# A decode layer on one core: five loop trips instead of four, a shorter TensorE program, 128 rows of w_down on 32 partitions, and unused products in TensorE's waits

## The chip, the cores and the metric

One core of one Trainium2 chip runs the kernel. The time is that of one execution on the device in microseconds (us). Times of the kernel before are the median of three runs; a profile is of one execution, whose own time is given beside its span.

The core has a matrix engine (TensorE, PE in the profile; PEld is its loading of weights), VectorE (DVE), ScalarE (ACT), GpSimd (POOL) and SyncE (SP), which here only issues transfers. Transfers run on sixteen DMA engines. Each engine follows its own program, and they wait for each other through semaphores.

## The reference

One step of decoding for two sequences: attention with a cache, then a gated feed-forward network, each behind a normalization and with its input added back. All arrays are bf16.

```python
B, Sq, D = 2, 1, 640;  Hq, Hkv, Sk, Dh = 32, 32, 8192, 192;  F = 1536
W = min(4096, max(256, Sk // 4))                     # 2048
xn = layernorm(x)
q = (xn @ wq).reshape(B, Sq, Hq, Dh).transpose(0, 2, 1, 3)
k, v = k_cache[:, :, Sk - W:, :], v_cache[:, :, Sk - W:, :]
p = softmax(einsum("bhqd,bhkd->bhqk", q, k) * Dh ** -0.5)
o = einsum("bhqk,bhkd->bhqd", p, v)
h = x + o.transpose(0, 2, 1, 3).reshape(B, Sq, Hq * Dh) @ wo
hn = layernorm(h)
out = h + (gelu(hn @ w_gate) * (hn @ w_up)) @ w_down
```

The last 2048 positions of K and V are read for each of 2 x 32 heads: 50.3 MB each. wq and wo are 7.9 MB each, w_gate, w_up and w_down 2.0 MB each.

## The kernel before

**Groups.** The 64 pairs of sequence and head are worked off in sixteen groups of four (`g`). A group is one K load and one V load of 3 MB each on 128 partitions: a partition holds 64 positions of one head, 24,576 bytes. Four groups form a round `J`, after which eight heads of both sequences are done.

**One group.** `transposes(g, half)` turns K by products with an identity (L574), six batches into four PSUM banks, which VectorE and ScalarE empty into `ktr` (L588, L584). `scores(g)` (L635) multiplies by the masked queries `rq`; VectorE finds the maxima (L644), a small product with `pm` (L651) spreads them, and ScalarE takes the exponentials (L655), all in `softmax`. `e_columns(g)` turns the exponentials into columns (L664), which VectorE masks into `ering`. `pv(g)` (L680) multiplies these with V and adds over the four groups of a round in the bank `ops`.

**The end of a round.** `z_rows` sums the exponentials, `o_rows` gathers the rows of the output through `osb` into the bank m1 (in the last round into `sps`), VectorE scales them into `orow`, `o_columns` (L713) turns them into columns `ot`, and `oproj(J)` (L731) multiplies with wo(J) into m1; VectorE adds the result to `hrow`.

**The queue of loads.** SP issues every large load (L363) in one fixed order. All of them share a ring of six slots of 24,576 bytes per partition: four for K (`K_AT`), two for V (`V_AT`), and other weights in slots that are free by then. A load is issued when the last reader of its bytes is done, so K waits for transposes and V for `pv`. wo(0) and wo(1) are loaded behind V of groups 3 and 7, wo(2) and wo(3) behind V of group 15, then w_gate, w_up and w_down. The first of five parts of w_gate and the two rows of x are issued by ScalarE at the start.

**The loop.** TensorE and VectorE run a loop of four trips; the other engines' programs are written out. Group 0's transposes, the queries (`q_rows`, L598, `q_stationary`) and group 0's scores and softmax stand ahead of it. A trip holds four groups as segments a to d; group `4J+p` does the first half of its transposes, `e_columns(g-1)`, the second half, `pv(g-1)`, its scores and its softmax. `o_columns` and `oproj` of the round before stand in segment a, under conditions on the trip, and the last trip leaves out d. The end of group 15, the last round, `oproj(2)` and `oproj(3)` stand behind the loop. Since a wait in the loop is a register that grows by a fixed step with each trip, every semaphore that is waited for there must be raised equally often in each trip; operations that don't fit get a semaphore class of their own (`cls`, `RARE`).

**The feed-forward part** follows `oproj(3)`. `h_columns` turns h into columns, `ffn_in` (L822) multiplies the normalized columns with w_gate, then w_up: for each of five parts of D, four products of 384 columns, one for each group of 32 columns of the array. `ffn_columns` (L831) turns the 98 x 384 results back into columns by three products of 128 columns, VectorE multiplies gelu's output with w_up's into `uT`, and 48 products (L871) with w_down in four pieces `WDC`, the last of one row per partition, end in m1. Each partition holds twelve rows of w_down. VectorE copies m1 to `yrow` (L877), and SP stores it.

## Time and profile before

| | us |
|---|---|
| median of 3 runs (292.71 to 292.77) | 292.76 |
| the profiled execution | 292.58 |
| its span | 291.3 |
| PE busy | 198.6 |
| DVE busy | 122.8 |
| ACT busy | 76.9 |
| POOL busy | 25.7 |
| DMA moved, mean over the span | 420 GB/s |

The span is from the first to the last instruction; the difference to the time lies around it. Busy time is the sum of an engine's instructions, and a busy engine isn't necessarily the bound. The mean granted clock of TensorE was 0.871 of full speed. Two more rows, from the costliest groups and from who waited for whom: the transposes (L574) took 116.2 us of TensorE's time in 768 products, and its products sat idle for 25.2 us until a K load landed. SP waited 130.5 us for `pv`, 35.4 us for transposes and 39.7 us for `oproj` before it could issue the next load.

### The profile page before, as it was taken

Reading aid. Unit: us, or ns where it says so; the run is one execution under the profiler, and the core shown is the slowest. Engines: PE = TensorE matmul, PEld = TensorE weight load, DVE = VectorE, ACT = ScalarE, POOL = GpSimd, SP = SyncE. Lnnn points to the kernel's source line nnn. Section 1 sums busy time; section 2 is a strip of 40 time slices with the busy share of each in tenths; the row PEclk is TensorE's granted clock in tenths of the full one; section 3 lists DMA queues with packets and bytes.
Section 4 is the critical chain, followed back from the end, with each engine's and each line's share of the span. In section 5 each row is a group of like instructions: output and inputs, shape, how many; then the busy total and the mean of one; then the engine's idle time right before and its main releaser. Section 6 shows DMA issues by size and latency. Waiting matters only on the chain.

```text
span 291.3 us, 5093 instructions
## 1 busy us (share of the span) xinstructions
PE 198.6 (68%) x2141; PEld 147.6 (51%) x2141; DVE 122.8 (42%) x231; ACT 76.9 (26%) x72; POOL 25.7 (9%) x85
## 2 busy tenths in 40 slices
PE   0650868786668288768677478868478778496684
PEld 0640437566355175637374475645465746472341
DVE  4350025455435334635356244635247445253331
ACT  1050014333322122423222123523142333151001
POOL 8820073000000000000000000000000000000000
PEclk9997568999979869997989579999689799688957
DMA  8999999999999999999999999999999999999994
GB/s 324 432 440 422 428 432 432 428 429 429 428 419 440 432 432 432 429 432 432 432 416 448 432 432 430 432 412 429 432 432 425 422 432 432 429 432 434 420 411 181
DMA packets 6506, 122.44 MB, mean 420 GB/s; under 512 B 734, under 2 KB 864, under 8 KB 1504
## 3 DMA queue, kind: packets, MB, share of 16 engines
q1 hardware_dynamic: 6348, 121.90, 97.8%
q10 hardware_dynamic: 148, 0.40, 0.4%
q8 instruction: 7, 0.11, 0.2%
q14 instruction: 3, 0.02, 0.0%
HBM read 122.29 MB, written 0.00 MB: 420 GB/s over the span
## 4 chain that ended last, share of the span: by engine, by line
DMA 73%; PE 18%; DVE 3%; issue 2%; SPq 2%; ACT 1%; DVEq 0%
DMA ring<-in_A_k_cache_dram 54%; PE tpp L574 13%; DMA ring<-in_A_wq_dram 10%; DMA ring<-in_B_w_down_dram 9%; DVE ktr L588 3%; PE tpp L598 2%; SPq L363 2%; PE ops L680 1%; DVE ering L428 1%; ACT ktr L584 1%; PE m L731 1%; PE m L713 1%; PE m L871 0%; PE m L694 0%; DVE yrow L877 0%
## 5 line engine op out<-in xcount | busy, mean ns | idle before, releaser
L574 PE MATMUL tpp<-identf,ring 128*128 128x128 f32 x768 | 116.2, 314 | 39.3 <-DMA ring<-in_A_k_cache_dram 25.2
L574 PEld LDWEIGHTS tpp<-identf,ring 128*128 128x128 f32 x768 | 102.8, 163 | 47.5 <-DMA ring<-in_A_k_cache_dram 26.5
L588 DVE COPY ktr<-tpp 128x2048 bf16<-128x2048 bf16 x64 | 78.4, 1224 | 91.4 <-PE tpp L574 91.4
L584 ACT ACTIVATE ktr<-tpp 128x2048 bf16<-128x2048 bf16 x32 | 60.1, 1877 | 94.9 <-PE tpp L574 94.9
L655 ACT ACTIVATE eexp<-sm,nm 128x512 bf16<-128x512 f32 x16 | 11.6, 722 | 71.7 <-DVE nm L653 71.7
L635 PE MATMUL sps<-ktr,rq 128*16 128x512 bf16 x384 | 25.7, 402 | 1.1 <-POOL rq L428 1.1
L680 PE MATMUL ops<-ring,ering 128*32 128x384 bf16 x512 | 25.0, 339 | 0.0
L644 DVE CUSTOM_DVE_ANT_1 sm<-sps,mska 128x512 f32<-128x512 f32 x16 | 11.0, 686 | 27.0 <-issue 27.0
L428 POOL TENSOR_TENSOR rq<-qs,mask 128x96 bf16<-128x96 bf16 x16 | 5.5, 354 | 175.6 <-PE sps L635 154.1
L680 PEld LDWEIGHTS ops<-ring,ering 128*32 128x32 bf16 x512 | 12.7, 99 | 8.5 <-issue 2.8
L635 PEld LDWEIGHTS sps<-ktr,rq 128*16 128x16 bf16 x384 | 8.9, 89 | 14.4 <-issue 5.5
L651 PEld LDWEIGHTS m<-mrhs,pm 128*128 128x128 bf16 x16 | 1.5, 96 | 22.9 <-DVE mrhs L424 22.9
L651 PE MATMUL m<-mrhs,pm 128*128 128x16 bf16 x16 | 2.9, 184 | 14.8 <-DVE mrhs L424 14.8
L598 PE MATMUL tpp<-ring,xnT 128*32 128x384 bf16 x80 | 6.1, 499 | 9.4 <-DMA ring<-in_A_wq_dram 9.4
L598 PEld LDWEIGHTS tpp<-ring,xnT 128*32 128x32 bf16 x80 | 3.4, 143 | 11.9 <-issue 9.6
L621 DVE CAST qs<-ops 128x384 bf16<-128x384 f32 x1 | 0.6, 558 | 15.8 <-PE ops L616 15.8
L428 DVE TENSOR_TENSOR ering<-m,mask 128x256 bf16<-128x256 f32 x16 | 6.6, 415 | 1.3 <-PE m L664 1.3
L713 PE MATMUL m<-selb,orow 128*128 128x2 bf16 x48 | 3.5, 200 | 5.2 <-DVE ering L428 4.5
L713 PEld LDWEIGHTS m<-selb,orow 128*128 128x128 bf16 x48 | 3.2, 159 | 6.0 <-DVE ering L428 4.9
L664 PE MATMUL m<-sel,eexp 128*128 128x64 bf16 x64 | 4.8, 200 | 1.2 <-ACT eexp L655 1.2
L494 PE MATMUL m<-identb,xrow 2*128 2x2 bf16 x5 | 0.3, 173 | 7.4 <-DMA xrow<-in_A_x_dram 7.4
L428 DVE TENSOR_TENSOR orow<-m,wm 128x1536 bf16<-128x1536 f32 x3 | 5.3, 1751 | 0.0
(127 smaller groups left out, 93.6 us busy)
## 6 DMA issues: line engine op xcount, KB each, us to landing
ring<-in_A_k_cache_dram SPq DMA_DIRECT2D x16, 3072.0 KB, 29.5
ring<-in_A_v_cache_dram SPq DMA_DIRECT2D x16, 3072.0 KB, 25.4
ring<-in_A_wq_dram SPq DMA_DIRECT2D x1, 7680.0 KB, 28.1
ring<-in_A_wo_dram SPq DMA_DIRECT2D x4, 1920.0 KB, 21.6
ring<-in_B_w_gate_dram SPq DMA_DIRECT2D x1, 1536.0 KB, 31.4
ring<-in_B_w_up_dram SPq DMA_DIRECT2D x1, 1536.0 KB, 21.9
ring<-in_B_w_down_dram SPq DMA_DIRECT2D x1, 960.0 KB, 24.3
ring<-in_B_w_down_dram SPq DMA_DIRECT2D x1, 480.0 KB, 25.0
```

What stands on the lines that cost most here:

```text
L363: P.op("sp", lambda e, v=v, src=src: e.dma_start(v, src), W=toks + [("sem", sem)], dma=sem)
L428: return lambda e: e.tensor_tensor(out=out, in0=a, in1=b, op=op)
L574: ins = e.transpose(tpp[bi][:, 512 * j + 128 * u:512 * j + 128 * (u + 1)], kv[:, off:off + 128], identf[:, :])
L584: act(lambda e, dst=dst, bv=bv: e.activation(out=dst, in_=bv, func=ACT.Copy), W=[("kt", half, k)], X=both)
L588: dve(lambda e, dst=dst, bv=bv: e.tensor_copy(dst, bv.rearrange("p (a x) -> p a x", a=2)), W=[("kt", half, k)], X=both, cls=0)
L598: ins = e.matmul(tps[0][32 * r:32 * (r + 1), 0:384], lhsT=xnT[:, c, 32 * J:32 * (J + 1)], rhs=wq[:, c, 1536 * J + 384 * r:1536 * J + 384 * ...
L635: ins = e.matmul(sps[32 * ch:32 * ch + 16, :], lhsT=rq[:, g % 4, k, :], rhs=ktr[:, k // 2, 1024 * ch + k % 2:1024 * (ch + 1):2], start=(k ...
L644: dve(lambda e: e.tensor_tensor_reduce(out=sm[:, :].rearrange("p (u x) -> p u x", u=4), in0=sps[:, :].rearrange("p (u x) -> p u x", u=4), ...
L655: act(lambda e: e.activation(out=eexp[:, :], in_=sm[:, :], func=ACT.Exp, bias=nm[:, 0:1], scale=1.0, accum_out=zr[:, g % 4:g % 4 + 1]), R= ...
L664: ins = e.matmul(o, lhsT=eexp[:, 128 * u:128 * (u + 1)], rhs=sel64[:, :], start=True, stop=True)
L680: ins = e.matmul(ops_[32 * r:32 * (r + 1), 0:384], lhsT=ering[:, g % 4, t, :], rhs=vv[:, 384 * t:384 * (t + 1)], start=(g % 4 == 0 and t < 4),
L713: ins = e.matmul(m2[:, 2 * kk:2 * kk + 2], lhsT=orow[:, :, kk:DH:12], rhs=selb[:, :], start=True, stop=True)
```

## The change

**Loop and program.** The loop has five trips. Trip J below 4 does all transposes of group 4J, then (in trip 0) the queries, later the scores and softmax of groups 4J to 4J+3 with what lies between. Trip J above 0 first ends the round before: `e_columns` and `pv` of group 4J-1, `z_rows`, `o_rows`, `oproj(J-2)`, `o_columns(J-1)`. What stood ahead of the loop and behind it for groups 0 and 15 is gone from there; only `oproj(3)` stays behind.

**Semaphores.** The counts of classes 1 and 2 on TensorE and VectorE start from a bias of 16 with their first rise, the count of `wo` from 32 by an increment that GpSimd makes, so that a register's value stays above zero in every trip. More operations get classes of their own.

**Loads.** wo(0), wo(1) and wo(2) are issued behind V of groups 7, 11 and 15. wo(2) lies in the fourth K slot, w_up in the third. w_down's last 128 rows are a load of their own, `wds`, four rows for each of partitions 0 to 31, ahead of eleven rows for every partition in pieces of five, three, two and one.

**Products.** `ffn_in` splits the fourth product into one of 256 and one of 128 columns, `ffn_columns` has nine products instead of three (the last four for the 128 rows on 32 partitions), `uT` has sixteen columns of pairs instead of twelve. w_down takes 16 products with `wds` and 44 instead of 48 with the rest. `o_rows` writes to m2. `keep_busy(n)` multiplies the identity with `qrow` n times into a bank where nothing reads it.

```diff
-RARE = ("oc", "op")
+BIAS = 16
+WO_BIAS = 32
+RARE = ("oc", "q", "y0")
...
-        if eng == "pe" and self.seg in RARE:
+        if self.seg == "op" and eng in LOOPED:
+            cls = 2
+        elif eng == "pe" and self.seg in RARE:
             cls = 1
...
-            ins.then_inc(sems[o.key()], 1)
+            ins.then_inc(sems[o.key()], 1 + BIAS if o.cls in (1, 2) and o.idx == 1 and o.eng in LOOPED else 1)
...
-WDC = ((0, 6), (6, 9), (9, 11), (11, 12))
+WDC = ((0, 5), (5, 8), (8, 10), (10, 11))
+NS = 11
...
-WO_AT = (K_AT[3], K_AT[3], K_AT[2], 0)
+WO_AT = (K_AT[3], K_AT[3], K_AT[3], 0)
+WU_AT = K_AT[2]
+WDS_AT = K_AT[1] + 12288
...
-            wd = B_w_down.rearrange("(q p s) n -> q p s n", p=128, s=6)
+            load("wds", WDS_AT, 8 * D, B_w_down[128 * NS:F, :].rearrange("(c a u) n -> a c (u n)", a=8, u=4), lambda v: v[0:32, :], "wds")
+            wd = B_w_down[0:128 * NS, :].rearrange("(p s) n -> p s n", s=NS)
...
-            if g % 4 == 3 and g < NG - 5:
-                load_wo(g // 4)
-        load_wo(2)
+            if g % 4 == 3 and g > 3:
+                load_wo(g // 4 - 1)
         load_wo(3)
...
+        def keep_busy(n, bank=tps[1], tok=("t", 1)):
+            def fn(e):
+                for k in range(n):
+                    ins = e.matmul(bank, lhsT=identb[:, :], rhs=qrow[:, :, :, :].rearrange("p a b d -> p (a b d)")[:, 0:bank.shape[1]],
+                                   start=True, stop=True, skip_group_check=True)
+                return ins
+
+            pe(fn, R=["identb", "qrow"], X=[tok])
...
+        for J in range(5):
+            if J < 4:
+                P.loop_seg("d0", J)
+                transposes(4 * J, 0)
+                transposes(4 * J, 1)
+            if J == 0:
+                P.loop_seg("q", J)
+                q_rows()
+                q_stationary()
+            else:
+                P.loop_seg("y0", J)
+                e_columns(4 * J - 1)
+                z_rows(J - 1)
+                pv(4 * J - 1)
+                keep_busy(3, m1[:, 0:DH], "m1")
+                o_rows(J - 1)
+            if J > 1:
+                P.loop_seg("op", J)
+                keep_busy(2, m1[:, 0:DH], "m1")
+                oproj(J - 2)
+            if J > 0:
+                P.loop_seg("oc", J)
+                o_columns(J - 1)
+            if J < 4:
+                P.loop_seg("a0", J)
+                scores(4 * J)
+                softmax(4 * J)
+                for g in range(4 * J + 1, 4 * J + 4):
+                    transposes(g, 0)
+                    e_columns(g - 1)
+                    transposes(g, 1)
+                    pv(g - 1)
+                    scores(g)
+                    if g == 4 * J + 3:
+                        keep_busy(4, m1[:, 0:DH], "m1")
+                    softmax(g)
+                    if g == 4 * J + 3:
+                        keep_busy(6, m1[:, 0:DH], "m1")
         P.loop_seg()
-        e_columns(15)
-        z_rows(3)
-        pv(15)
-        o_rows(3)
-        oproj(2)
-        o_columns(3)
+        keep_busy(1)
         oproj(3)
+        keep_busy(2)
...
+                        for r in range(3):
+                            e.matmul(bank[32 * r:32 * r + 2, 0:384], lhsT=hnT[:, c, :], rhs=cols[:, :, 3 * r:3 * r + 3],
+                                     start=(c == 0), stop=(c == NC5 - 1), tile_position=(0, 32 * r))
+                        e.matmul(bank[96:98, 0:256], lhsT=hnT[:, c, :], rhs=cols[:, :, 9:11], start=(c == 0), stop=(c == NC5 - 1),
+                                 tile_position=(0, 96), skip_group_check=True)
+                        ins = e.matmul(bank[96:98, 256:384], lhsT=hnT[:, c, :], start=False,
+                                       rhs=wv[:, c - l0, 128 * NS:F].rearrange("p (c a u) -> p a c u", c=4, a=8),
+                                       stop=(c == NC5 - 1), tile_position=(0, 96), skip_group_check=True)
...
-                    ins = e.transpose(bank[:, 128 * j:128 * j + 98], row[0:98, j:384:3], identf[0:98, 0:98])
+                    e.transpose(bank[:, 128 * j:128 * j + 66], row[0:66, j:384:3], identf[0:66, 0:66])
+                for j in range(2):
+                    e.transpose(bank[:, 128 * j + 96:128 * j + 98], row[96:98, j:256:2], identf[96:98, 96:98])
+                for u in range(4):
+                    ins = e.transpose(bank[0:32, 384 + 32 * u:386 + 32 * u], row[96:98, 256 + u:384:4], identf[96:98, 96:98])
...
+        order = [(None, 4, ["d0", (None, 1, ["q"])]), (0, None, ["y0", (1, None, ["op"]), "oc"]), (None, 4, ["a0"])]
+        P.emit_loop("dve", nc.vector, sems, 5, order)
+        P.emit_loop("pe", nc.tensor, sems, 5, order)
```

More of the change, by code (lines that the diff above doesn't have):

```diff
@@ L159, in resolve @@
         for e, l in self.per.items():
-            n = {}
+            n = {c: BIAS for c in (1, 2) if e in LOOPED}
             for o in l:
@@ L607, in q_rows @@
                 in_=tps[0][:, 0:384].rearrange("p (h d) -> p h d", h=2).unsqueeze(2).to_broadcast([128, 2, 2, DH]),
-                func=ACT.Copy, scale=SCALE), W=["qrow"], X=[("t", 0)])
+                func=ACT.Copy, scale=SCALE), W=["qrow"], X=[("t", 0)], cls=1)
         def q_stationary():
@@ L752, in h_columns @@
             pe(fn, R=["hrow", ("hsel", 0), ("hsel", 1)], X=["m2"])
-        transposes(0, 0)
-        transposes(0, 1)
-        q_rows()
-        q_stationary()
         consts_late()
-        scores(0)
-        softmax(0)
-        for J in range(4):
-            for p in range(1, 5 if J < 3 else 4):
-                g = 4 * J + p
-                seg = "abcd"[p - 1]
-                P.loop_seg(seg + "0", J)
-                transposes(g, 0)
-                e_columns(g - 1)
-                if p == 4:
-                    z_rows(J)
-                if p == 1 and J > 0:
-                    P.loop_seg("oc", J)
-                    o_columns(J - 1)
-                P.loop_seg(seg + "1", J)
-                transposes(g, 1)
-                if p == 1 and 0 < J < 3:
-                    P.loop_seg("op", J)
-                    oproj(J - 1)
-                P.loop_seg(seg + "2", J)
-                pv(g - 1)
-                scores(g)
-                if p == 4:
-                    o_rows(J)
-                softmax(g)
@@ L819, in fn @@
                     for c in range(c0, c1):
[L820 to L823 removed]
+                        cols = wv[:, c - l0, 0:128 * NS].rearrange("p (x s) -> p x s", s=NS)
+                        for r in range(3):
[6 more added lines that the diff above has]
+                                       stop=(c == NC5 - 1), tile_position=(0, 96), skip_group_check=True)
                     return ins
@@ L863, in bass_sequential_preLN__sliding_block_cached__geglu_ffn__decode_kernel, with wds_rows @@
         vT = ffn_columns(urow, [("osb", 0), ("osb", 1)], tps[1], 1)
-        dve(tt(uT[:, :, 0:17:16].rearrange("p (r j) b -> p r j b", r=4), vT, rjb(ga[:, 0, :]), ALU.mult), R=["ga0"], W=["uT"], X=[("t", 1)])
+        dve(tt(uT[:, :, 0:17:16], vT, kb(ga[:, 0, :]), ALU.mult), R=["ga0"], W=["uT"], X=[("t", 1)])
+        wds, wtoks = where["wds"]
+        def wds_rows(e):
+            for u in range(4):
+                for r in range(4):
+                    ins = e.matmul(m1[32 * r:32 * r + 17, 0:160], lhsT=uT[0:32, 12 + u, 0:17], rhs=wds[:, D * u + 160 * r:D * u + 160 * (r + 1)],
+                                   start=False, stop=False, tile_position=(0, 32 * r), skip_group_check=True)
+            return ins
+        pe(wds_rows, R=["uT"] + wtoks, X=["m1"])
         for i, (f0, f1) in enumerate(WDC):
```

76 lines of the change are left out of this document (36 added, 40 removed).

## The prediction

> **What bounds the kernel now.** I read the rows by slice first, then the queues, the chain of waits, the last microseconds of the DMA by windows, and the timeline of the tail.
>
> ```profile
> DMA  8999999999999999999999999999999999999994
> GB/s 324 432 440 422 428 432 432 428 429 429 428 419 440 432 432 432 429 432 432 432 416 448 432 432 430 432 412 429 432 432 425 422 432 432 429 432 434 420 411 181
> q1 hardware_dynamic: 6348, 121.90, 97.8%
> q8 instruction: 7, 0.11, 0.2%
> ...
> DMA 73%; PE 18%; DVE 3%; issue 2%; SPq 2%; ACT 1%; DVEq 0%
> ```
>
> The DMA engines are full in every slice but the first and the last, at about 430 GB/s: TensorE, busy 68% of the span, waits for K rather than the other way round. So a change can only save at the start, at the end, in the bytes, or by how evenly the sixteen engines finish. Queue q8 is code: seven packets, 0.11 MB, so 16 KB each.
>
> ```profile
> 262.97 25.38 DMA ring<-in_B_w_down_dram
> 288.35 0.04 issue
> 288.39 0.75 PE m L871 x11
> 289.14 0.02 issue
> 289.17 0.32 DVE yrow L877
> ```
>
> The chain ends in one long landing, then 0.8 us of work. By half microseconds, the DMA share in the last but one column:
>
> ```profile
> core 0: us, PE busy (x) PEld busy (x) DVE busy (x) ACT busy (x) POOL busy (x), PEclk, DMA share, GB/s
> 286.00:286.50 0.50, 0.07 (x1) 0.02 (x1) 0.22 (x1) 0.00 (x0) 0.00 (x0) 1.00 0.94 361
> 286.50:287.00 0.50, 0.49 (x24) 0.39 (x24) 0.00 (x0) 0.00 (x0) 0.00 (x0) 1.00 0.63 241
> 287.00:287.50 0.50, 0.10 (x8) 0.00 (x0) 0.00 (x0) 0.00 (x0) 0.00 (x0) 1.00 0.57 209
> 287.50:288.00 0.50, 0.39 (x12) 0.18 (x12) 0.00 (x0) 0.00 (x0) 0.00 (x0) 0.85 0.34 128
> 288.00:288.50 0.50, 0.10 (x7) 0.11 (x8) 0.00 (x0) 0.00 (x0) 0.00 (x0) 0.50 0.15 54
> ```
>
> The end is ragged: the share falls from 0.94 at 286.5 to 0.15 at 288.5, that is from fifteen engines to two. In idle engine time that is 0.5 x (0.06 + 0.37 + 0.43 + 0.66 + 0.85) = 1.19 us, the most that evening out could save. The trace also holds the sixteen rises of each load's semaphore, one for each engine. For the last load they lie at 286.89 to 288.76: six engines within 0.14 us of the first, five alone at 0.34, 0.58, 0.69, 1.00 and 1.50 us behind, and five at 1.72 to 1.87. For the load of wq, landed at 29.58, the spread is 0.60 us. It grows to 1.75 after the first code packet (33.4 us in the trace), and with each packet after it (54.4, 64.4, 76.2, 92.7) one more engine stands 1.7 us or more behind; the packet at 275.1 makes the engine at 1.50, the one at 287.4 shows in no rise. So a code packet holds back one engine by about 1.5 us, a different one each time, the DMA never pauses to let it catch up, and the last engine sets the end.
>
> **The change, part by part.**
>
> *The w_down rows.* Every engine now carries 8 partitions x 12 rows of 1,280 B. After, it carries 8 x 11, that is 10,240 B less, and 164 KB go in a load of their own, whose source has an outermost step of 8. This trace has two loads with a short outermost step: x (2) and the output (4). Their semaphores rise only two and four times after the first jump, against sixteen for 128 partitions, so I take eight engines for a step of 8. At 430 / 16 = 26.9 GB/s, 10,240 B are 0.38 us: eight engines end 0.38 us earlier, and the eight with 20,480 B more end 0.38 us later. Which eight are late the trace doesn't name. The two engines that carried x can be followed packet by packet: neither can have taken any of the five code packets of the loop. If short loads start at the same engines, two of the eight that get more rows are early ones. I take the case in which all late ones are among the other eight: -0.38 us. Bound on the other side: +0.38.
>
> [...] No run here loads 32 partitions; but the engines finish every late load here up to 1.9 us apart and still start the next one at once, so I keep -0.38.
>
> *The shorter program.* The built TensorE program has 762 products instead of 858, so 7 x 762 / 858 = 6.2, six code packets instead of seven. One that falls away takes one engine out of the late group, not the group: 0 us, and up to -0.15 us (1.87 less 1.72) if it was the last one's.
>
> *The fifth trip.* Transposes, scores and the tail's work on group 15 move into the loop. At each group of four both halves of the transposes now precede e_columns, pv(4J-1), oproj and o_columns. What releases buffers is pv for V and the transposes for K; both keep their places within a few products. In the SP queue wo moves: now after v7, v11 and v15, and the third needs K_AT[3], so it waits for the transposes of group 15. Those end at 261.16 (the w_up issue at 261.18, released by the same products, shows it). v15 is landing until 266.48, so the queue still holds 5.3 us when wo is issued, 3.4 for the engine that is first by 1.9. The only row for issue to first data is the start, 0.72 to 1.73 for wgh, 1.0 us. Cost 0; without that cover, the 1.0 us would show. Behind wo stand wo3, w_gate, w_up and w_down, eight or nine issues of 0.3 to 0.6 us; they are out by about 267 with at least 9 us queued ahead of them. In the middle, wo of trip 2 lands 4.6 us after v7, and scores(8) stand behind it; k9 lands 7.3 us later still, so this fills a wait for K (25.2 us of such waits on L574).
>
> *The unused products.* 58 of 192 columns in the loop, three of 512 outside. The nearest rows give 0.18 us each (L651), above the 0.1 to 0.2 that the columns ask for by L680 (32 of 384 columns, four side by side, in 1.48). Four before the wait of L651 for mrhs take 0.7 us, where that product waits 1.08 us; six after it end while the next K is landing; the others stand where osb and orow take 0.62 and 1.76 us on VectorE. Cost 0. Two of 512 columns behind oproj(3) take 0.4 us at the full clock and 0.9 at half, against a wait of 0.60 us for rs: 0 to +0.25. Their gain, a warmer clock (0.50 granted from 277.6 to 284.4), is bounded by the products it would shorten, below.
>
> *The tail's products.* These are the rows:
>
> ```profile
> 282.44 0.77 PE L831 MATMUL tpp<-identf,sm 98*128 98x98 f32 x3 [0.20 <-DVE sm L424]
> 283.13 1.67 PE L822 MATMUL ops<-ring,hnT 128*2 128x384 bf16 x20
> 285.49 0.59 PE L831 MATMUL tpp<-identf,osb 98*128 98x98 f32 x3 [0.69 <-ACT osb L861]
> 286.51 0.59 PE L871 MATMUL m<-ring,uT 128*17 128x160 bf16 x24 [0.44 <-DMA ring<-in_B_w_down_dram]
> 288.80 0.10 PEld L871 LDWEIGHTS m<-ring,uT 128*17 128x17 bf16 x4 [0.29 <-DMA ring<-in_B_w_down_dram]
> ```
>
> w_up and w_gate get five products a step instead of four for the same columns: 0 to +0.1 each. Each turn into columns gets nine instead of three: two more with 128 columns (0.21 us by L831's weights) and four with 32 (0.065 by L748's), +0.68; bounds 0.39 (all by L748) and 1.26 (all by L831). uT ended at 286.33; at half clock it now ends at 286.33 + 2 x 0.68 + 0.1 = 287.8, with a warm clock nearer 286.4, since w_up itself lands at 283.06 and 284.03. Then come 60 products instead of 48, at 25 to 33 ns by the rows of L871: 1.5 to 2.0 us. Warm, TensorE reaches the last piece before it lands (288.76 - 0.38 = 288.38), and its last four products (288.80 to 289.11 at half clock) shorten by about 0.07 us. Cold, they end at 289.3 to 289.8, against 289.11 now. I take the warm end, since the added products fill exactly the windows in which the clock fell: -0.07.
>
> *Semaphore counts, their biases, one increment on GpSimd*: 0, under GpSimd's 265 us of idle time.
>
> **Sum:** -0.38 - 0.07 = -0.45 us. The profiled execution took 292.58 us (span 291.3 and 1.3 around it), so 292.13; its 0.18 below the median 292.76 carries over: **292.31 us**, its own range 291.9 to 292.7. A measurement of this kernel tells 0.2%, 0.59 us, from no change; the faster side begins at 292.17, so this case straddles it.
>
> **The rivals.**
> *The removed packet is the last one's.* For: five engines lie within 0.15 us, and one packet goes. Against: any of the others may be the one. -0.45 - 0.15 = -0.60, 292.16 and below.
> *A late engine is among the eight.* For: three of the five are as likely here as there by what the trace names. Against: the two x engines are clean. +0.38 at the DMA's end, which hides TensorE: 293.1.
> *TensorE's tail becomes the end (slower).* Place: the two turns into columns and the 60 products. If a short transpose costs what a long one does and the clock stays at 0.50, uT ends at 286.33 + 2 x 1.26 + 0.35 = 289.2, the products at 291.2: +2.1 us. With the middle price of 0.68 and the slow products it is +0.7 (289.8 against 289.11). It decides from uT at about 287.3 on. 293.4 to 294.9. For: this chain already met w_up within 0.1 us. Against: 0.5 to 1 us of slack behind uT, and the clock.
> *The loop no longer stays in TensorE's memory (slower).* It grows from some 475 products to 582, with jumps over 362 of them in the last trip. If code came again in each trip, each engine hit twice would stand another 1.5 us behind: 294.3 or more. Against: nothing came on q8 between 92.7 and 275.1, over three trips.
> [...]
>
> **How the numbers follow.** Forecast 0.55 (0.25 of it below 292.17, 0.30 above), the removed packet 0.13, a late engine among the eight 0.13, TensorE's tail 0.12, code again 0.07. Faster: 0.25 + 0.13 = 0.38. Same: 0.30 + 0.13 + 0.02 (the tail at its lowest) = 0.45. Slower: 0.10 + 0.07 = 0.17. The range 291.8 to 293.6 takes in both signs of the 0.38 us and the tail's low price; it leaves out code again and the tail's high price.
>
> **What would show it.** Right: six packets on q8, the new load's semaphore rising eight times, the rises of the last load ending near 288.4, DMA share 0.9 until about 286.9. Wrong: a slice of the DMA row below 9 near 264 us (wo too late); uT after 287.3 or products of w_down that follow the last landing back to back; code packets between 100 and 270 us; a last rise later than 288.8.

## The result and the profile after

The changed kernel takes 294.47 us (median of 6 runs, 294.30 to 294.83), the kernel before in the same rounds 292.66 us (6 runs, 292.48 to 292.77). The ratio is 1.0065, with an interval of 1.0055 to 1.0076: slower by 1.81 us. The forecast of 292.31 us and its range, 291.8 to 293.6, both miss it. The profiled execution took 294.49 us, its span is 293.2.

Two lines of the page of after, the code queue and the chain of waits by engine:

```profile
q8 instruction: 6, 0.10, 0.1%
...
DMA 58%; PE 24%; DVE 7%; issue 5%; ACT 4%; SPq 1%; DVEq 0%
```

Six code packets came, as forecast. But the chain that ended last is the DMA's for 58% of the span, where it was 73%, and PE's share rose from 18 to 24%. The end of the same chain of after, in order of time (start, length, what it was):

```profile
260.88 14.77 DMA ring<-in_A_wo_dram
276.11 1.70 PE m L746 x23
279.01 1.25 PE m L763 x20
289.47 1.60 PE m L911 x44
```

Before, the chain's last transfer was w_down's. Now it is wo's at 275.65, and everything behind it is compute. Rows of the timeline of before's tail (start, busy time, engine, line; in brackets the idle time in front and what ended it), then of after's; the weight loads are left out in both:

```profile
271.89 0.29 PE L726 MATMUL m<-xrow,identb 2*2 2x320 bf16 x2
...
275.86 0.99 PE L731 MATMUL m<-ring,ot 128*2 128x320 bf16 x24 [1.16 <-DMA ring<-in_A_wo_dram]
279.19 0.17 DVE L428 TENSOR_TENSOR hnT<-m,mean 128x10 bf16<-128x10 f32 x1 [1.08 <-PE m L748]
286.11 0.22 DVE L428 TENSOR_TENSOR uT<-tpp,ga 128x24 bf16<-128x24 f32 x1 [1.01 <-PE tpp L831]
```

```profile
275.69 0.42 PE L741 MATMUL m<-xrow,identb 2*2 2x320 bf16 x2 [2.58 <-DMA ring<-in_A_wo_dram]
276.04 1.77 PE L746 MATMUL m<-ring,ot 128*2 128x320 bf16 x24
277.74 1.03 PE L669 MATMUL tpp<-qrow,identb 128*128 128x512 bf16 x2
...
280.28 0.17 DVE L436 TENSOR_TENSOR hnT<-m,mean 128x10 bf16<-128x10 f32 x1 [1.08 <-PE m L763]
...
287.36 0.61 PE L857 MATMUL tpp<-identf,osb 66*128 66x66 f32 x3 [0.67 <-ACT osb L891]
287.90 0.40 PE L859 MATMUL tpp<-identf,osb 2*128 2x2 f32 x2
288.16 0.27 PE L861 MATMUL tpp<-identf,osb 2*32 2x2 f32 x4
288.46 0.24 DVE L436 TENSOR_TENSOR uT<-tpp,ga 128x32 bf16<-128x32 f32 x1 [1.69 <-PE tpp L861]
288.76 0.71 PE L900 MATMUL m<-ring,uT 32*17 32x160 bf16 x16 [0.34 <-DVE uT L436]
289.40 1.65 PE L911 MATMUL m<-ring,uT 128*17 128x160 bf16 x44
291.10 0.33 DVE L917 CAST yrow<-m 113x160 bf16<-113x160 f32 x1 [2.39 <-PE m L911]
```

wo(3) lands when it did (at 275.64; before at 275.72). The products of `oproj(3)` with wo start 0.18 us later and take 1.77 us for 0.99. They start later because two products that add the input x (L741 above, L726 in before) have moved: in before they belong to `oproj(2)` and run ahead of the wait for wo(3), in after to `oproj(3)` and run behind it. The description of the change doesn't mention this, and no run here undoes it by itself. hnT comes at 280.28 instead of 279.19, uT starts at 288.46 instead of 286.11. The 44 products of w_down have no idle time in front: the last piece had landed at 288.80, and they end at 291.05. yrow starts 1.93 us later than before, which is the whole difference of the two profiled executions (294.49 and 292.58 us).

The 1.09 us to hnT are the later start (0.18), `oproj(3)` at half clock (0.78) and the rest (0.13), in which the two unused products stand, also at half clock. From hnT to uT it is 1.26 us more: 0.19 in w_gate, 0.30 in the first turn (1.07 for 0.77), 0.30 in w_up, 0.48 in the second turn (1.07 for 0.59), less 0.01 elsewhere. Behind uT, 60 products take 2.29 us and nothing covers them. Why the clock matters here, in steps of 3.41 us (span of the step, then busy time of each engine, the granted clock, the DMA's share and GB/s), of after:

```profile
core 0: us, PE busy (x) PEld busy (x) DVE busy (x) ACT busy (x) POOL busy (x), PEclk, DMA share, GB/s
...
269.56:272.97 3.41, 2.24 (x41) 1.37 (x38) 2.31 (x3) 0.00 (x0) 0.00 (x0) 1.00 1.02 432
272.97:276.38 3.41, 0.83 (x11) 0.30 (x14) 0.12 (x1) 0.00 (x0) 0.00 (x0) 0.50 0.97 410
276.38:279.80 3.42, 3.42 (x44) 1.93 (x36) 0.66 (x3) 0.00 (x0) 0.00 (x0) 0.50 1.00 424
279.80:283.21 3.41, 3.14 (x43) 1.85 (x43) 0.81 (x5) 0.46 (x2) 0.00 (x0) 0.50 0.99 407
283.21:286.62 3.41, 3.23 (x39) 1.86 (x34) 1.78 (x8) 0.23 (x1) 0.00 (x0) 0.50 0.98 387
```

The granted clock falls to 0.50 at 272.97, ahead of `oproj(3)`, and stays there to the end. Before, it was 1.00 from 270.79 to 277.61 and again from 284.44 to 287.85. TensorE is busy for 92 to 100% of the last three steps shown and gets no more clock for it. The same columns of before, for two steps at 0.50 and the one at 1.00 that follows:

```profile
277.61:281.02 3.41, 3.14 (x40) 2.15 (x44) 0.80 (x5) 0.30 (x2) 0.00 (x0) 0.50 0.96 405
281.02:284.44 3.42, 3.22 (x43) 1.18 (x31) 1.43 (x6) 0.38 (x2) 0.00 (x0) 0.50 1.02 417
284.44:287.85 3.41, 1.80 (x47) 1.02 (x39) 0.81 (x4) 0.58 (x1) 0.00 (x0) 1.00 0.80 312
```

The DMA ends where it did. The rises of two semaphores in after, in us, each rise one engine (the first line is the second load of w_up, on all sixteen; the second is `wds`, whose semaphore had risen once before, at 263.98, which is read here as the eight engines that carry nothing of it):

```
wu1  282.09 282.10 282.11 282.18 282.23 282.27 282.34 282.36 282.80 282.86 283.23 283.67 283.69 283.84 283.85 284.00
wds  282.87 282.90 282.97               283.57 283.65 284.02 284.46 284.48
```

The rises of `wds` match eight of the first line at a distance of 0.76 to 0.79 us: three of the first four (282.09 to 282.18), then 282.80, 282.86, 283.23, 283.67 and 283.69. The last two belong to the late five. So two of the five late engines got the additional rows. In w_down's last load they end at 288.79 and 288.80, the other three at 288.20 to 288.37, the first engine at 286.53 (286.89 before).

### The profile page after: what moved, and what is told of

Same layout as the page of the kernel before. It is cut to its first block, busy times and chain, and to the rows that moved or that the text cites. A ratio compares the mean times of both kernels' runs of the same rounds, so it can differ in the third digit from the quotient of the medians.

```text
span 293.2 us, 5379 instructions
## 1 busy us (share of the span) xinstructions
PE 203.7 (69%) x2236; PEld 148.6 (51%) x2236; DVE 124.1 (42%) x232; ACT 76.9 (26%) x72; POOL 25.8 (9%) x85
## 4 chain that ended last, share of the span: by engine, by line
DMA 58%; PE 24%; DVE 7%; issue 5%; ACT 4%; SPq 1%; DVEq 0%
DMA ring<-in_A_k_cache_dram 43%; PE tpp L581 11%; DMA ring<-in_A_wq_dram 10%; DMA ring<-in_A_wo_dram 5%; DVE ktr L595 4%; PE ops L696 3%; ACT ktr L591 3%; PE tpp L605 2%; DVE orow L436 1%; PE m L720 1%; PE m L746 1%; SPq L371 1%; DVE ering L436 1%; PE m L728 1%; PE m L911 1%
## 5 line engine op out<-in xcount | busy, mean ns | idle before, releaser
L581 PE MATMUL tpp<-identf,ring 128*128 128x128 f32 x768 | 111.3, 304 | 37.2 <-DMA ring<-in_A_k_cache_dram 19.8
L581 PEld LDWEIGHTS tpp<-identf,ring 128*128 128x128 f32 x768 | 96.7, 157 | 48.2 <-DMA ring<-in_A_k_cache_dram 21.3
L605 PE MATMUL tpp<-ring,xnT 128*32 128x384 bf16 x80 | 5.5, 457 | 9.4 <-DMA ring<-in_A_wq_dram 9.4
L436 DVE TENSOR_TENSOR orow<-m,wm 128x1536 bf16<-128x1536 f32 x4 | 7.0, 1758 | 3.6 <-PE m L720 3.6
L669 PE MATMUL m<-qrow,identb 128*128 128x192 bf16 x58 | 7.5, 253 | 0.0
L669 PEld LDWEIGHTS m<-qrow,identb 128*128 128x128 bf16 x58 | 4.4, 98 | 3.6 <-issue 3.4
```

The lines of the kernel that those rows point to most:

```text
L436: return lambda e: e.tensor_tensor(out=out, in0=a, in1=b, op=op)
L581: ins = e.transpose(tpp[bi][:, 512 * j + 128 * u:512 * j + 128 * (u + 1)], kv[:, off:off + 128], identf[:, :])
L605: ins = e.matmul(tps[0][32 * r:32 * (r + 1), 0:384], lhsT=xnT[:, c, 32 * J:32 * (J + 1)], rhs=wq[:, c, 1536 * J + 384 * r:1536 * J + 384 * ...
L669: ins = e.matmul(bank, lhsT=identb[:, :], rhs=qrow[:, :, :, :].rearrange("p a b d -> p (a b d)")[:, 0:bank.shape[1]], start=True, stop=Tru ...
```

## The experiments

Theory A: the end is TensorE's chain from wo(3) on, and its length is set by the split's added products and by the granted clock. Rivals: B, the uneven load moves the DMA's end; C, the loop of five trips costs by itself. Each group of runs shares runs of the kernel before, with medians of 292.63, 292.68 and 292.66 us.

**After without the split.** w_down, w_gate, w_up and the turns are as before, the loop and the unused products as in after.

```diff
-WDC = ((0, 5), (5, 8), (8, 10), (10, 11))
+WDC = ((0, 6), (6, 9), (9, 11), (11, 12))
...
-            load("wds", WDS_AT, 8 * D, B_w_down[128 * NS:F, :].rearrange("(c a u) n -> a c (u n)", a=8, u=4), lambda v: v[0:32, :], "wds")
-            wd = B_w_down[0:128 * NS, :].rearrange("(p s) n -> p s n", s=NS)
+            wd = B_w_down.rearrange("(q p s) n -> q p s n", p=128, s=6)
```

> The changed kernel with w_down, w_gate's and w_up's products and the turns into columns as before (five trips, unused products and wo's new places stay). Theory A (TensorE's products behind the last wo set the end, and both the half clock and the added products lengthen them): the six products less in each turn save 0.30 and 0.48 us, five instead of four products a step in w_up some 0.1 us, and 48 instead of 60 last products at 38 ns 0.45 us, 1.3 us in all: 293.2 us, still above before. Rival B (the split alone makes the loss): 292.7. Rival C (the fifth trip and the code it loads make the loss): 294.4.

Measured: 292.90 us (292.33 to 293.32, 11 runs), ratio 1.0007 [0.9999, 1.0016]. Between A's figure and B's, by A's mechanism: the last landing is at 288.52, and in this run's timeline w_down's 48 products follow uT without a gap at half clock.

```profile
275.70 1.75 PE L745 MATMUL m<-ring,ot 128*2 128x320 bf16 x24
...
287.10 0.22 DVE L435 TENSOR_TENSOR uT<-tpp,ga 128x24 bf16<-128x24 f32 x1 [1.29 <-PE tpp L851]
287.37 1.78 PE L891 MATMUL m<-ring,uT 128*17 128x160 bf16 x48 [0.32 <-DVE uT L435]
289.21 0.33 DVE L897 CAST yrow<-m 113x160 bf16<-113x160 f32 x1 [1.89 <-PE m L891]
```

So the split is needed for the loss, and the loop is not the loss (C falls). With the same half clock, yrow starts at 289.21 here and at 291.10 in after, 1.89 us apart. Of this, 0.34 is the earlier start of `oproj(3)` in this execution (275.70 for 276.04; wo(3) landed at 275.43). From there on the split is worth 1.55 us of a chain at half clock, and it is worth 1.57 us of the medians.

**After without the three unused products of 512 columns.**

```diff
-        keep_busy(1)
         oproj(3)
-        keep_busy(2)
```

> The changed kernel without the three unused products of 512 columns outside the loop. Theory A: the two behind oproj(3) hold the next product back by 0.2 us, so 294.3 us, clock unchanged at 0.50. If they held the clock up anywhere, later products get longer: 294.6 or more. Rivals B and C: no change, 294.5.

Measured: 294.00 us (293.20 to 294.53, 6 runs), ratio 1.0047 [1.0032, 1.0061]. In the profiled execution the clock was 1.00 until 276.78, `oproj(3)` took 0.99 us, and yrow started at 290.19 for 291.10. This is one of the faster executions: three lie at 293.20 to 293.58, three at 294.43 to 294.53. The intervals of this ratio and of after's overlap: the clock was higher without the three products in this execution, and whether they cost anything is not told. A expected an unchanged clock.

**Before with the split alone.** The four-trip loop, with w_down, w_gate, w_up and the turns of after (the reverse of the first diff).

> The kernel before with the split of w_down alone (own load of 128 rows on 32 partitions, its products and turns into columns). Theory A: uT, 286.33 us before, comes some 1.1 us later, then 60 products take 1.6 to 2.3 us and end at 289.0 to 289.7 instead of 289.11: 292.6 to 293.3 us, since part of the tail keeps the full clock. Rival B: 294.4. Rival C: 292.3 (the forecast's gain) to 293.0 (the last landing 0.38 us later).

Measured: 293.39 us (292.98 to 294.46, 7 runs), ratio 1.0038 [1.0024, 1.0052]. Slower although the last products of the profiled execution have the full clock, and just above A's range. Four of the runs lie at 292.98 to 293.39 and three at 294.19 to 294.46; the profiled one, at 292.98, is the fastest. Its timeline:

```profile
287.92 0.24 DVE L430 TENSOR_TENSOR uT<-tpp,ga 128x32 bf16<-128x32 f32 x1 [1.47 <-PE tpp L842]
288.22 0.45 PE L881 MATMUL m<-ring,uT 32*17 32x160 bf16 x16 [0.33 <-DVE uT L430]
288.60 0.94 PE L892 MATMUL m<-ring,uT 128*17 128x160 bf16 x44
289.59 0.33 DVE L898 CAST yrow<-m 113x160 bf16<-113x160 f32 x1 [1.43 <-PE m L892]
```

Here the 60 products take 1.37 us, from 288.22 on, against 2.29 in after. The clock was 0.50 from 265.86 to 282.93, so uT came late all the same.

**After with more unused products.** Six more ahead of `oproj` in the loop, seven more ahead of `oproj(3)`.

```diff
-                keep_busy(2, m1[:, 0:DH], "m1")
+                keep_busy(8, m1[:, 0:DH], "m1")
                 oproj(J - 2)
...
-        keep_busy(1)
+        keep_busy(8)
         oproj(3)
```

> The changed kernel with eight instead of two unused products ahead of oproj in the loop and eight of 512 columns instead of one ahead of oproj(3), while it waits for wo. Theory A, if unused products can hold the clock: the clock stays at 1.0 past 275.7 us, oproj(3) takes 1.0 us instead of 1.8, and the end comes 0.8 to 1.5 us earlier: 293.0 to 293.7 us. If the clock stays at 0.50 all the same: 294.5 to 294.8. Rivals B and C: 294.5.

Measured: 292.83 us (292.06 to 293.34, 11 runs), ratio 1.0003 [0.9995, 1.0012]. More work on TensorE, and the loss is gone, by more than A expected. The clock holds until 278.40, uT starts at 287.19, and the profiled execution, at 293.22, has half clock from 278.40 on. The mean granted clock of every run is on record: it is 0.900 to 0.927 here and 0.877 to 0.899 in after.

**Eight ahead of oproj(3) only.** The second half of that diff alone, on after.

> After, with eight unused products of 512 columns instead of one ahead of oproj(3), nothing else. Theory A (the clock of the tail fell in the step of 3.41 us in which TensorE waits for the last wo): the granted clock is 1.0 through oproj(3), which then takes 0.98 us and not 1.77, and the time is that of the run with more unused products, 292.6 to 293.2. Rival K (it takes the loop's products too): the clock stays at 0.50, 294.2 to 294.6.

Measured: 293.09 us (292.31 to 293.50, 11 runs), ratio 1.0015 [1.0006, 1.0024]. The clock is 1.00 from 270.49 to 280.73, and in the timeline the wait for wo(3) has shrunk:

```profile
275.68 0.30 PE L741 MATMUL m<-xrow,identb 2*2 2x320 bf16 x2 [0.40 <-DMA ring<-in_A_wo_dram]
275.90 0.99 PE L746 MATMUL m<-ring,ot 128*2 128x320 bf16 x24
```

K falls: the eight products ahead of `oproj(3)` do most of it. The idle time ahead of `oproj(3)` was 1.16 us in before, 2.58 in after, 2.67 in after without the split; it is 0.40 here. The fifth trip does the last round's work earlier (`ot` is ready at 273.09 instead of 274.92), and TensorE stands idle longer ahead of wo(3). Whether this wait is what takes the clock is not settled. For it: without the split and with sixteen engines (below), the clock falls at the end of the step that holds most of the wait (0.74 and 0.84 us of work in 3.41). Against it: in after the clock fell at 272.97, and the wait began at 273.11; without the three products of 512 columns TensorE waited 2.00 us, and the clock stayed at 1.00 to 276.78.

**No split, more unused products.** The first and the fourth edit together.

> The loop and the program of after, w_down, w_gate, w_up and the turns as before, and eight unused products instead of two ahead of oproj in the loop and eight instead of one ahead of oproj(3). Theory A (the end is TensorE's chain from wo3 on, and its length is set by the split's added products and by the granted clock): without the split the chain is 1.2 to 1.6 us shorter, and with a clock of 1.0 up to about 278 (as the run of after with more unused products had it) uT comes at about 286.2 to 286.6 and the products of w_down wait for the last landing again: 292.3 us (292.1 to 292.6). Rival E (the clock of the tail does not matter once the split is gone): as the run without the split, 292.9. Rival F (unused products only take time): above 293.2. Last landing 288.5 to 288.9 by all.

Measured: 292.59 us (292.44 to 292.73, 11 runs), ratio 0.9998 [0.9989, 1.0007], at the top of A's range and with the mechanism that A names: uT starts at 286.17, and w_down's last twelve products wait for a landing at 288.61. More unused products are worth some 0.3 us without the split (the two intervals overlap), against 1.6 with it, and the spread of the runs falls from 1.0 to 0.3 us.

**Unused products in before.** The four-trip kernel, with `keep_busy` added.

```diff
+        keep_busy(8)
         oproj(3)
+        keep_busy(2)
```

> Before, with eight unused products of 512 columns ahead of oproj(3) and two behind it, nothing else. Theory A: before ends with its last landing, so a warmer tail is worth nothing: 292.6 within 0.2%, and uT moves up while w_down's products wait for the landing as before. Rival H (before too is bound by TensorE's tail in part): 292.2 or below. If the products in front delay oproj(3) and the clock is not held: 292.9 to 293.3.

Measured: 292.55 us (292.39 to 292.75, 11 runs), ratio 0.9998 [0.9989, 1.0007]: no change. But uT did not move up either (286.24 for 286.11). Before had the full clock in `oproj(3)` already, and here the eight products put it back to 276.48 from 275.86. The clock, at 1.00 until 281.22, made that good, but not more: w_up's products start at 283.22, where their load has just landed (283.17).

**Unused products through the whole tail.** On the run with more unused products, eight more of 512 columns.

```diff
+        keep_busy(2, tps[3], ("t", 3))
         ffn_in(sps, "s", "wg", ((0, 1), (1, 2)), ((0, 1), (1, NC5)))
...
+        keep_busy(2, tps[3], ("t", 3))
         gT = ffn_columns(grow[:, 0:384], ["sm"], tps[0], 0)
...
+        keep_busy(1, tps[3], ("t", 3))
         ffn_in(ops_, "o", "wu", WUC, WUC)
...
+        keep_busy(2, tps[3], ("t", 3))
         vT = ffn_columns(urow, [("osb", 0), ("osb", 1)], tps[1], 1)
...
+        keep_busy(1, tps[3], ("t", 3))
         wds, wtoks = where["wds"]
```

> The run of after with more unused products, and eight unused products of 512 columns more in the tail: two ahead of w_gate, two ahead of its turn, one ahead of w_up, two ahead of its turn and one behind uT's, all on a bank that nobody reads any more. Theory A: the clock is held by full products, so it stays at 1.0 to about 287 or later, the turns take 0.7 instead of 1.07 us, uT comes at 286.4 to 287.0, the 60 products take 1.5 us and the last ones wait for the last landing: 292.3 us (292.1 to 292.6). Rival G (the clock falls anyway): each of the eight takes 0.43 us at half clock, some 3.4 us of which the waits hide about 2: 293.8 to 294.5.

Measured: 293.37 us (292.70 to 293.81, 6 runs), ratio 1.0026 [1.0013, 1.0039]. Between the theories. In the profiled execution, at 292.94, the clock does come back, 1.00 from 282.19 to the end, and w_down's 60 products take 1.32 us. But where TensorE had no wait to fill, the unused products are queue: hnT is ready at 279.25, and w_gate starts at 279.94 behind this row.

```profile
279.37 0.63 PE L669 MATMUL tpp<-qrow,identb 128*128 128x512 bf16 x1 [0.33 <-DVE dT L436]
```

w_up starts at 284.36, for 283.45 in the run with more unused products, uT at 287.87.

**Unused products ahead of the turns only.** Two of the five edits.

```diff
+        keep_busy(2, tps[3], ("t", 3))
         gT = ffn_columns(grow[:, 0:384], ["sm"], tps[0], 0)
...
+        keep_busy(2, tps[3], ("t", 3))
         vT = ffn_columns(urow, [("osb", 0), ("osb", 1)], tps[1], 1)
```

> The run of after with more unused products, with two unused products of 512 columns ahead of each of the two turns into columns, where TensorE waits 0.7 us. Theory A: nothing is queued ahead of w_gate and w_up as in the run with eight of them, so w_up starts at 283.4 again, the clock comes back to 1.0 at about 282, uT comes at 286.9 to 287.2, the products of w_down reach the last piece before it lands: 292.3 to 292.7, with less spread than the 1.3 us of the run without them. Rival G (each unused product only takes time): 293.0 to 293.6.

Measured: 292.59 us (292.52 to 292.78, 11 runs), ratio 1.0001 [0.9992, 1.0010]. A's case, within its range, and with a spread of 0.26 us for 1.28. The steps of the clock in this run:

```profile
core 0: us, PE busy (x) PEld busy (x) DVE busy (x) ACT busy (x) POOL busy (x), PEclk, DMA share, GB/s
...
279.34:282.75 3.41, 3.08 (x36) 1.67 (x38) 1.02 (x4) 0.47 (x2) 0.00 (x0) 0.50 0.99 407
282.75:286.17 3.42, 3.36 (x37) 1.80 (x36) 1.48 (x7) 0.80 (x2) 0.00 (x0) 1.00 1.01 407
286.17:289.58 3.41, 2.50 (x69) 1.88 (x69) 0.57 (x2) 0.02 (x1) 0.00 (x0) 1.00 0.32 119
```

uT starts at 287.30, but the products run warm, and yrow starts at 289.13, 0.34 us behind the last landing at 288.79. Five trips, the split and 60 products are all there, and cost nothing with the clock at 1.00 in the last 7 us. They gain nothing either. The clock came back at 282.75, just as the first pair began (282.68), so this profile alone does not show that the pair did it; the narrow spread of eleven runs is what speaks for it.

**Other numbers of engines for the 128 rows.** On after, an outermost step of 16, as below; on the run with more unused products, and on the last one, a step of 4 (a=4 and c=8 in the same places).

```diff
-            load("wds", WDS_AT, 8 * D, B_w_down[128 * NS:F, :].rearrange("(c a u) n -> a c (u n)", a=8, u=4), lambda v: v[0:32, :], "wds")
+            load("wds", WDS_AT, 8 * D, B_w_down[128 * NS:F, :].rearrange("(c a u) n -> a c (u n)", a=16, u=4), lambda v: v[0:32, :], "wds")
...
-                                       rhs=wv[:, c - l0, 128 * NS:F].rearrange("p (c a u) -> p a c u", c=4, a=8),
+                                       rhs=wv[:, c - l0, 128 * NS:F].rearrange("p (c a u) -> p a c u", c=2, a=16),
```

> After, with the 128 rows loaded with an outermost step of 16 instead of 8, so that two partitions instead of four go to each engine. The semaphore of wds then rises sixteen times instead of eight. Theory A (TensorE's chain sets the end): nothing changes, 294.2 to 294.6, and w_down's products again follow each other back to back. What it tells of the DMA: no engine gets more than another, so the last rises of w_down stand where the late engines of before stood, 288.6 to 288.9, and the spread of the last load falls back from 2.3 to about 1.9 us. Rival B (the uneven load is what costs): 293.6 to 294.0.

> The run of after with more unused products, with an outermost step of 4 in the load of the 128 rows: eight partitions each on four engines, so that the other twelve carry 10,240 B less than in before. The semaphore of wds rises four times. Theory I (the step of 8 won nothing because two of the five late engines were among the eight): if the four are early engines, the last landing moves up by 0.38 us to 288.4 to 288.6; if a late one is among them, it lands 1.1 us later, at 289.9. Rival J (the 32 partitions take the data no faster whatever the number of engines): all engines are held up and the last landing is 289.5 or later with every engine behind. The time follows only if TensorE is done by then: 292.4 to 292.9 with early engines, 293.7 with a late one.

> The last two together: unused products ahead of the turns, and the 128 rows on four engines. If theories A and I both hold, the last landing is at 288.4 and TensorE is not behind it: 292.0 to 292.4, the fastest of all. If I fails (a late engine among the four): 293.5 to 293.9. If A fails: 293.0 to 293.6.

Measured: with sixteen engines 293.88 us (293.69 to 294.36, 5 runs), ratio 1.0043 [1.0030, 1.0057]; with four 294.18 us (294.11 to 294.31, 5 runs), 1.0053 [1.0039, 1.0067]; with four and the warm turns 294.06 us (294.01 to 294.28, 5 runs), 1.0049 [1.0035, 1.0063]. In the first, the median lies in B's range and not in A's, but what B supposes, an earlier end of the DMA, is not there: in the profiled execution, at 294.36 in A's range, TensorE sets the end (uT starts at 288.30, yrow at 290.94). An execution that TensorE doesn't hold up would start yrow 0.41 us behind the landing at 290.06, 0.47 us sooner, which as an estimate gives 293.89, close to the median. In the two with four engines the DMA sets the end, and both lie above every time that was expected for them. Neither theory expected the last landing of the first run: 290.06 with sixteen, and 290.46 and 290.50 with four, against 288.80 with eight. Two of the microseconds in which the rows are loaded, of after, of sixteen and of four:

```profile
283.00:284.00 1.00, 0.82 (x11) 0.29 (x3) 0.62 (x1) 0.00 (x0) 0.00 (x0) 0.50 1.03 418
284.00:285.00 1.00, 1.00 (x14) 0.71 (x17) 0.18 (x1) 0.00 (x0) 0.00 (x0) 0.50 1.00 405
```

```profile
283.00:284.00 1.00, 0.82 (x8) 0.43 (x3) 0.48 (x1) 0.00 (x0) 0.00 (x0) 0.50 0.90 280
284.00:285.00 1.00, 1.00 (x17) 0.75 (x19) 0.32 (x2) 0.00 (x0) 0.00 (x0) 0.50 1.09 287
```

```profile
283.00:284.00 1.00, 1.00 (x17) 0.75 (x19) 0.35 (x2) 0.00 (x0) 0.00 (x0) 0.50 1.18 299
284.00:285.00 1.00, 1.00 (x20) 0.60 (x12) 0.60 (x5) 0.23 (x1) 0.00 (x0) 0.50 0.96 236
```

The engines are about as busy (the last column but one) and move 28 to 42% less (the last). With four, even the first of the sixteen engines ends 1.3 us later (287.83 for 286.53). So J's event came, and not I's: with this form of the load all engines were held up. The reason that J gives doesn't hold: with eight engines the others were not held up (in after the first engine of the last load ends at 286.53, in before at 286.89). Whether a load that misses the five late engines would win the 0.38 us is not settled by these runs, since both changed more than which engines carry the rows.

**All profiled executions beside each other**, in us, with the time of the profiled execution and the median of the kernel's runs at the right. The two can differ by up to 0.48 us:

| | clock in oproj(3) | uT starts | clock of w_down's products | last landing | yrow starts | profiled | median |
|---|---|---|---|---|---|---|---|
| before | 1.00 | 286.11 | 1.00, 0.50 | 288.76 | 289.17 | 292.58 | 292.66 |
| after | 0.50 | 288.46 | 0.50 | 288.80 | 291.10 | 294.49 | 294.47 |
| no split | 0.50 | 287.10 | 0.50 | 288.52 | 289.21 | 292.72 | 292.90 |
| no unused products of 512 columns | 1.00 | 287.55 | 0.50 | 288.82 | 290.19 | 293.58 | 294.00 |
| split alone | 0.50 | 287.92 | 1.00 | 288.81 | 289.59 | 292.98 | 293.39 |
| more unused products | 1.00 | 287.19 | 0.50 | 288.92 | 289.83 | 293.22 | 292.83 |
| no split, more unused | 1.00 | 286.17 | 0.50 | 288.61 | 289.02 | 292.44 | 292.59 |
| sixteen engines | 0.50 | 288.30 | 0.50 | 290.06 | 290.94 | 294.36 | 293.88 |
| unused through the tail | 1.00 | 287.87 | 1.00 | 288.77 | 289.55 | 292.94 | 293.37 |
| unused in before | 1.00 | 286.24 | 1.00, 0.50 | 288.87 | 289.28 | 292.69 | 292.55 |
| four engines | 1.00 | 287.23 | 0.50 | 290.46 | 290.87 | 294.24 | 294.18 |
| eight ahead of oproj(3) | 1.00 | 286.89 | 1.00, 0.50 | 289.05 | 289.46 | 292.86 | 293.09 |
| warm turns | 1.00 | 287.30 | 1.00 | 288.79 | 289.13 | 292.52 | 292.59 |
| warm turns, four engines | 1.00 | 287.50 | 1.00, 0.50 | 290.50 | 290.91 | 294.28 | 294.06 |

Where the DMA sets the end, yrow starts 0.34 to 0.41 us behind the last landing. Where TensorE does, yrow starts 2.64 us behind uT at half clock with 60 products (after, no unused products of 512 columns, more unused products, sixteen engines), 1.67 to 1.68 at full clock (split alone, unused through the tail), 2.11 at half clock with 48 (no split). No run beats before by more than a measurement tells.

## Why the prediction was wrong

**The step that failed** is the one on the tail's products: "I take the warm end, since the added products fill exactly the windows in which the clock fell: -0.07." The clock was at its cold end from 272.97 on. Of the three unused products outside the loop one ran ahead of `oproj(3)` (0.38 us) and two behind it, at half clock already (1.03 us, for the 0.9 that the forecast estimated); none stood in the 10 us that follow. The split's own products did fill them, TensorE was busy for 3.14 to 3.42 us of each step of 3.41 from 276.38 to 286.62, and the clock stayed at 0.50 all the same. The step also looked at the windows in which the clock of before fell, from 277.6 on; in after it fell at 272.97, ahead of `oproj(3)`. Why it fell there stays open. The fifth trip makes the idle time ahead of wo(3) 2.58 us for 1.16, but in after this wait began only behind the fall. Costing the trip at nothing was right for the loads and the loop (no split with more unused products: 0.9998). The forecast itself put the cold end at 289.3 to 289.8 for the last product; it was 291.05. Two delays were not in that sum at all: 0.78 us for `oproj(3)` at half clock and 0.18 for the products with x ahead of it. Of what was in it, w_gate and w_up took 0.39 more and the 60 products 0.29 more, the turns 0.58 less.

**The price of the turns** was too high and that of the 60 products too low. A turn costs 0.30 us more at half clock (1.07 for 0.77) and 0.44 more at full (1.03, in the run with warm turns, for 0.59), not 0.68. The prices by the nearest rows, L831 and L748, were right: the two added products of 128 columns take 0.39 to 0.40 us together and the four of 32 columns 0.27, at either clock (0.42 and 0.26 in the forecast). What the sum left out is that the three parts of a turn overlap by 0.20 us (0.57, 0.39 and 0.27 in 1.03, warm turns), and that at half clock the first three products, now of 66 rows, take 0.61 us for 0.77. w_gate and w_up cost 0.19 and 0.30 us more instead of at most 0.1 each. The 60 products take 2.29 us cold and 1.37 warm, not 2.0 and 1.5.

**The rival was right.** "TensorE's tail becomes the end" had 0.12 and 293.4 to 294.9 us; it was 294.47. Its place, the turns and the 60 products, holds in part: of the 2.35 us by which uT starts later, 0.78 lie in the turns, 0.49 in w_gate and w_up, and 1.09 ahead of hnT, where the rival saw nothing. The clock, which it names as against it, came out on its side. That its high sum, 291.2 us for the last product, lies near the measured 291.05 is luck: it took 1.26 us more for each turn, which cost 0.30 and 0.48. Its point of decision, uT at about 287.3, lies between two: from the table, uT has to end by about 286.8 at half clock (289.17, less 2.64, and 0.24 for uT itself) and by 287.7 at full clock.

**The DMA's end.** -0.38 us rested on all five late engines lying among the eight that get nothing more. Two lay in the other eight. The three that didn't moved by about 0.4 us (to 288.37 from 288.76), but the two late ones among the eight had stood only 0.31 us in front of the last, and 0.76 us more put them behind it. The end went from 288.76 to 288.80. The rival of a late engine among the eight had the right event and the wrong size, +0.38, since it took the very last engine for it: less 0.31, that is 0.07, and 0.04 was measured. In after the load of the 128 rows took its eight engines 0.76 to 0.79 us, for the 0.76 that 20,480 B give at the forecast's 26.9 GB/s; the other eight did not wait for it, since the first engine of the last load moved from 286.89 to 286.53, by 0.36 of the 0.38 us.

**Right:** six code packets on q8 and eight late rises of the new load; no gap near 264 us (the DMA's share was 0.97 and 1.11 in the microseconds from 263 and from 264); no code packet on q8 between 80.7 and 286.2 us, so no code came for the later trips of the loop of 582 products. The packet that fell away is the one that came at 275.1 us in before, which had made none of the five late engines late: no gain, as the main case had it.

## What to carry to other kernels

When two chains end within half a microsecond of each other, price both for each edit at both clocks, from the last common event on; here the edit was to take 0.38 us from the one, and it put some 1.5 us on the other at half clock. Products added for the clock belong where TensorE waits: here, ahead of the turns they cost nothing that the runs show (292.59 us, for 292.83 without them), and through the whole tail, ahead of w_gate too, some of them were only queue (293.37). And look at the packets of all loads when the outermost step of one is changed: with steps of 16 and 4 for the 128 rows the 6,400 B packets beside them took up to 534 and 526 ns, with a step of 8 at most 259.

## What the runs showed of the hardware

**In these runs the granted clock is not a matter of busy time alone.** It changes in steps of 3.41 us: in the traces of before and after, each stretch of one clock ahead of the last lasts 3.41 us or a multiple of it. At 0.50, steps in which TensorE was busy for 3.08 us (warm turns), 3.15 (split alone), 3.22 (before, 281.02 to 284.44) and 3.23 (eight ahead, 280.73 to 284.14) were followed by 1.00. Steps of 3.14, 3.23 and 3.42 us in after, and of 3.14 and 3.42 in after without the split, were followed by 0.50 again. What decides it stays open: no run here changes the kind of product alone, and without the split the tail has before's products and stayed at 0.50. The steps lie differently in each profiled execution. Kernels that TensorE can end spread over 1.0 to 1.5 us (no split, more unused products, eight ahead, split alone), after itself over 0.5, before and those that behave like it over 0.3 to 0.6. That the place of the steps makes the spread is an argument: of the unprofiled runs only the mean clock is on record, and it is lower in the slower runs without the split (0.897 and more below 292.75 us, 0.894 and less above), but higher in the slower ones of the split alone.

**With steps of 16 and 4, the load of the 128 rows slowed the packets beside it.** Packets of 5,120 B, which only this load has, took 202 ns on average in after, 206 at most. With sixteen engines they took up to 418 ns and with four up to 416, and the 6,400 B packets of w_down beside them, 248 ns on average in after, 259 at most, up to 534 and 526. Only the step of 8 left the packets beside it as they were: 6,400 B in 248 ns are 25.8 GB/s for an engine, and the 7,680 B packets of w_down in before, at 296 ns, have 25.9. Why the packets slow each other is not shown here.
